# Five small loads moved from SyncE to ScalarE, and 26 filling products, at the start of an attention and routing kernel

## Chip, cores and metric

The kernel runs on one core of a Trainium2 chip. The time is that of the whole program on the device, in microseconds (us); lower is better. A time of a kernel is the median of several executions; one more execution was recorded by the profiler, and all rows of the trace come from that one.

## What is computed

Pooled attention is followed by a mixture of experts in which every token goes to one expert. Batch is 8, heads 8, sequence 576, head width 64; there are 8 experts, 4608 tokens of width 512, and 1024 hidden units per expert.

```python
k_p = k.reshape(B, H, Sp, 8, D).mean(axis=3)      # keys and values averaged over 8 rows
v_p = v.reshape(B, H, Sp, 8, D).mean(axis=3)
scores = scale * q @ k_p^T ; attn = softmax(scores) ; x = attn @ v_p
logits = x @ w_gate + modality_bias[modality_id]   # the five loads bring modality_id and modality_bias
e_idx = argmax(logits) ; gate_w = softmax(logits)[e_idx]
out[token] = gate_w * (relu(x @ w1[e_idx]) @ w2[e_idx])
```

## The kernel before

**Stages.** The attention takes the first 145 us or so. It runs in 20 steps, five for each pair of batches. A step takes one or two tiles of 128 queries: `q_pe` turns the queries (L679), `q_act` copies them out (L685), `s_pe` makes the scores (L704, L698), `s_dve` takes the maximum and subtracts it (L711, L714), `s_act` is the exponential (L726, L727), `t_pe` and `t_act` turn the weights (L733, L738), `a_pe` multiplies by the values (L768, L772), `x_dve` divides (L801). The rest of the span is the experts, on TensorE.

**Keys and values.** For each batch the 8 rows of a block are added up: by `fold` on GpSimd (POOL, L458 to L460) or by `reduce8` on VectorE (DVE, L463). `k_operand` then turns the pooled keys (L502, L507) and ScalarE copies them (L510, L511). `v_operand` lets ScalarE scale the pooled values (L542, L543), TensorE turn them (`pv`, L549: three transposes, u = 0, 1, 2) and ScalarE copy the result (L551). `gate_operand` (L444, L446) lays out the gate weights `wg` on GpSimd.

**Order.** Every engine runs its own instructions in the order in which the program lists them. SyncE (SP) issues all loads and stores: before the first step the loads of batches 0 and 1, the gate weights and one mixed tile of queries (L360 to L395, L439), then by `step_loads` what each step asks for. The five loads of `load_routing` stand in step 1, after the loads for q 2, k 3 and v 3 and before that for k 4. They bring the token's modality in two parts for each half of a batch pair (L583: 128 partitions by 4 pieces of 32 bytes; L585: 64 partitions by 4 pieces of 8 bytes) and the bias table for all partitions (L588: 128 pieces of 64 bytes). Their only reader is `modality_terms` on GpSimd in step 5 (L624 to L627).

**Turns.** The framework gives each load or store that SyncE or ScalarE issues one of eight completion semaphores, in turn over both engines in the order of its schedule, and a load first waits until the load that had its semaphore before it has landed.

**Filling.** `fill(n)` (L490) issues n products of 128 by 128 by 128 in bf16 on constants into a PSUM tile that nobody reads. The opening lines up to the step loop (L1070 to L1086) and two of its helpers have 58 of them (L494).

Of the kernel before, what the change touches and what calls it, by code (L numbers as in the profile page):

```python
# [9 lines left out]
F32 = mybir.dt.float32  # L10
# [12 lines left out]
P = 128  # L23
# [11 lines left out]
def kernel(  # L35
# [303 lines left out]
    with ExitStack() as actx:  # L339
# [150 lines left out]
        def fill(n):  # L490

            t = ps_av.tile([P, 2, 512], F32, tag="av", name="fill")
            for _ in range(n):
                nc.tensor.matmul(t[:, 0, 0:P], iota_b, iota_b, start=True, stop=True)  # L494

        def k_operand(b, i):
            kp, kp4 = kps[b]
            dst = kt[b % NB]
            pk = ps_tr.tile([64, 3 * P], F32, tag="tr", name=f"pk_{b}_{i}")
            cs = K_PART[i]  # L500
            for j, c in enumerate(cs):
                nc.tensor.transpose(pk[:, j * P:(j + 1) * P], kp[:, c, :], ident)  # L502
                if b == 0 and i == 0:
                    fill(5 if j else 20)
            n = len(cs) * P
            if i == 1:
                nc.tensor.transpose(pk[:, n:n + P], kp[:, NCH, :], ident)  # L507
                n += 64
            x = slice(cs[0] * P, cs[0] * P + n)
            nc.scalar.copy(dst[0:64, 0, x], pk[:, 0:n])  # L510
            nc.scalar.copy(dst[64:128, 1, x], pk[:, 0:n])  # L511
# [27 lines left out]
        def v_operand(b):  # L539
            vp, vp4 = vps[b]  # L540
            dw, d4 = vw[b % NB], v4[b % NB]
            nc.scalar.activation(dw[:, :, 0, 0:HD], vp[:, 0:NPAIR, :], AF.Copy, scale=m_a)  # L542
            nc.scalar.activation(dw[:, :, 1, 0:HD], vp[:, 0:NPAIR, :], AF.Copy, scale=m_b)  # L543
            (nc.gpsimd if b else nc.vector).tensor_tensor(d4[:, :, 0:HD], vp4.rearrange("p (o d) -> p o d", o=1).to_broadcast([P, NPAIR, HD]),
                                    m4b.to_broadcast([P, NPAIR, HD]), op=ALU.mult)

            pv = ps_tr.tile([P, 3, P], F32, tag="tr", name=f"pv_{b}")
            for u in range(3):
                nc.tensor.transpose(pv[:, u, :], vp[:, 2 * u:2 * u + 2, :], ident)  # L549
            vts[b] = ap.tile([P, 3, P], F32, tag="vt", bufs=1, name=f"vt_{b}")  # L550
            nc.scalar.copy(vts[b], pv)  # L551

# [21 lines left out]

        RC = {}

        def load_routing():

            mod = ap.tile([P, NT, 2], I32, name="mod")
            mv = modality.bitcast(I32).rearrange("(n w) -> n w", w=2)  # L580
            for z in range(2):
                mz = mv.rearrange("(i z s) w -> z i s w", z=2, s=S)[z]
                nc.sync.dma_start(mod.rearrange("p (i t) w -> p i (t w)", t=GT)[:, :, 10 * z:10 * z + 8],  # L583
                                  mz[:, 0:512, :].rearrange("i (p j) w -> p i (j w)", j=4))
                nc.sync.dma_start(mod.rearrange("p (i t) w -> p i t w", t=GT)[64 * z:64 * z + 64, :, 4, :],  # L585
                                  mz[:, 512:S, :].rearrange("i p w -> p i w"))
            mb = ap.tile([P, 2, E], F32, name="mb")
            nc.sync.dma_start(mb.rearrange("p m e -> p (m e)"),  # L588
                              modality_bias.rearrange("m e -> (m e)").rearrange("(o x) -> o x", o=1).to_broadcast([P, 2 * E]))
            RC.update(mod=mod, mb=mb)  # L590

        def routing_constants():
            ids = ap.tile([P, NT], I32, name="ids")
# [75 lines left out]
        def q_pe(n, w):  # L669
            b, jj, ts_ = steps[n]  # L670
            nq = 2 * len(ts_)
            qt = ap.tile([P, 4, P], F32, tag=f"qt{w}", bufs=1, name=f"qt_{n}_{w}")
            pq = ps_tr.tile([P, 4, P], F32, tag="tr", name=f"pq_{n}_{w}")
            for c in range(nq):
                if jj is None:
                    src = qmix[b // 2][:, 4 * w + 2 * c:4 * w + 2 * c + 2, :]
                else:
                    src = qpure[b][:, 4 * w + c, 2 * jj:2 * jj + 2, :]
                nc.tensor.transpose(pq[:, c, :], src, ident)  # L679
            qts[n, w] = qt  # L680
            pqs[n, w] = pq[:, 0:nq, :]

        def q_act(n, w):
            pq = pqs.pop((n, w))
            nc.scalar.copy(qts[n, w][:, 0:2 * len(steps[n][2]), :], pq)  # L685
# [62 lines left out]
        def t4_act(n):  # L748

            dst = pt4s[n]  # L750
            for z in range(len(steps[n][2])):
                nc.scalar.copy(pt4z[z][64 * z:64 * z + 64], dst[64 * z:64 * z + 64])  # L752
# [298 lines left out]

        step_loads = {}
        for n, fn, b in ((0, load_k, 2), (0, load_k4, 2), (0, load_v, 2), (0, load_v4, 2), (1, load_q, 2), (1, load_k, 3),
                         (1, load_v, 3), (1, load_k4, 3), (1, load_routing, None), (1, load_k, 4), (2, load_qmix, 1),
                         (2, load_v4, 3), (2, load_v, 4), (3, load_k4, 4), (4, load_q, 3), (4, load_k, 5), (4, load_v4, 4),
                         (4, load_v, 5), (5, load_k4, 5), (5, load_k, 6), (6, load_q, 4), (6, load_v4, 5), (6, load_v, 6),
                         (7, load_qmix, 2), (7, load_k4, 6), (7, load_k, 7), (9, load_q, 5), (9, load_v4, 6), (9, load_v, 7),
                         (10, load_k4, 7), (11, load_q, 6), (11, load_v4, 7), (12, load_qmix, 3), (14, load_q, 7)):
            step_loads.setdefault(n, []).append((fn, b))
# [11 lines left out]
        k_operand(0, 0)  # L1071
        q_pe(0, 0)
        q_act(0, 0)
        fill(6)
        s_pe(0, 0)
        fill(14)
# [1 line left out]
        s_dve(0, 0)  # L1078
        token_ids()
        k_operand(0, 1)  # L1080
        q_pe(0, 1)
        q_act(0, 1)
        pool_v(0)
        gate_operand()
        fill(8)
        s_act(0, 0)  # L1086

        def run(hook, n):
            for fn in hook.get(n, ()):
# [7 lines left out]
        for n in range(N + 1):  # L1097
            has, nxt, nxt2 = n < N, n + 1 < N, n + 2 < N
            old = steps[n - 1][2] if n else ()
            two = len(old) > 1  # L1100
            ahead = two and has and steps[n][1] is None
            loads(n)
            run(hook_0, n)
            if old:
                t_pe(old[0])
                t_act(old[0])
                if has:
                    s_act(n, 0)
            if has:
                s_pe(n, 1)  # L1110
            if due:
                release()
            if old:
                t4_pe(n - 1)
                t4_act(n - 1)
            if n == N:
                run(hook_3, N - 1)
            if ahead:
                t_pe(old[1])
                t_act(old[1])  # L1120
            if n == 2:
                a_pe(old[0])
            run(hook_1, n)
            if old and n != 2:
                a_pe(old[0])
            if has:
                s_dve(n, 1)
            finish()
            if n == 0:
                q_pe(1, 0)  # L1130
                q_act(1, 0)
                v_operand(0)
            if two and not ahead:
                t_pe(old[1])
                t_act(old[1])
            if n == 1 or n == 2:
                q_pe(n + 1, 0)
                q_act(n + 1, 0)
            if nxt:
                q_pe(n + 1, 1)  # L1140
            run(hook_q, n)
            if old:
                x_dve(old[0])
            if n == N - 2:
                finish()
            gap(2)
            if nxt and n:
                q_act(n + 1, 1)
            if has:
                s_act(n, 1)  # L1150
            if n == 0:
                q_act(n + 1, 1)
            if n == 1:
                pool_k_rest(1)
                pool_v_rest(1, 2)
                a_pe(old[1])
                x_dve(old[1])
            if n == 2:
                pool_k_rest(2, 2)
            if nxt:  # L1160
                s_pe(n + 1, 0)
            if nxt2 and n > 1:
                q_pe(n + 2, 0)
                q_act(n + 2, 0)
            if nxt:
                s_dve(n + 1, 0)
            if n == 2:
                pool_k_rest(2)
            if n == 0:
                v_gate(0)  # L1170
                pool_k(1)
            run(hook_2, n)
            finish()
            due = bool(drip) and drip[0] in held
            if two and n != 1:
                a_pe(old[1])
                x_dve(old[1])
            gap(2)
            if n != N - 1:
                run(hook_3, n)  # L1180
            finish()
# [557 lines left out]
```

## Time and profile before

| | us |
|---|---|
| median of three executions | 581.89 |
| lowest and highest of the three | 579.84, 583.59 |
| the profiled execution, its own time | 581.18 |
| its span in the trace, first to last instruction | 579.5 |
| TensorE busy in it | 562.1 (97%) |
| mean granted TensorE clock | 0.996 |

The profiled execution lies 0.7 us under the median, and 1.7 us of its time lie outside the span. Times in the trace count from the start of the span. PE is TensorE, PEld its weight loads, DVE VectorE, ACT ScalarE, POOL GpSimd, SP SyncE; SPq is an instruction of SyncE's own queue, here the issue of a load. A tile's name stands without its number: `qt` is any of the query tiles. The granted clock is a share of 2.4 GHz, so 0.50 is 1.2 GHz.

### The profile page before, as it was taken

The page shows a single profiled execution, that of the slowest core. Times are in us where ns is not written, and L with a number is a line of the kernel's source. Part 1 is how long each engine was busy: PE and PEld are TensorE (multiplying, and loading weights), DVE is VectorE, ACT ScalarE, POOL GpSimd, SP SyncE. Part 2 cuts the span into 40 slices and gives each one's busy share as a digit, 9 for nine tenths or more (in the row PEclk, how much of TensorE's full clock was granted, in tenths as well). Part 3 has the DMA queues.
Part 4 walks back from the last instruction along what each step waited for, and adds up shares of the span by engine and source line. Part 5 has one row for each costly group of instructions (what it writes and reads, how often), then busy time and mean ns, then how long its engine had stood idle before and what let it go on. Part 6 is the DMA issues. An engine that isn't in the chain of part 4 may idle for free.

```text
span 579.5 us, 12256 instructions
## 1 busy us (share of the span) xinstructions
PE 562.1 (97%) x3487; PEld 494.5 (85%) x3487; DVE 372.7 (64%) x947; ACT 270.7 (47%) x656; POOL 183.6 (32%) x292
## 2 busy tenths in 40 slices
PE   4999999999999999999999999999999999999996
PEld 4889889899898888888888888888888888888894
DVE  5887888778878786567455446855455588455311
ACT  2667667789752443334333336533333474334210
POOL 6679987854201302202202102022112113212102
PEclk9899999999999999999999999999999999999999
DMA  8998999994431533232232277233234853242001
GB/s 249 279 332 251 358 334 281 338 274 164 166 94 43 153 101 111 79 105 94 92 110 95 89 236 244 93 114 94 87 114 129 241 205 108 91 133 74 26 21 56
DMA packets 80940, 90.69 MB, mean 157 GB/s; under 512 B 17935, under 2 KB 56335, under 8 KB 80848
## 3 DMA queue, kind: packets, MB, share of 16 engines
q1 hardware_dynamic: 74928, 70.14, 39.3%
q0 software_dynamic: 5920, 19.44, 10.3%
q8 instruction: 43, 0.70, 0.5%
q14 instruction: 49, 0.40, 0.3%
HBM read 115.72 MB, written 28.62 MB: 249 GB/s over the span
## 4 chain that ended last, share of the span: by engine, by line
PE 90%; DVE 3%; DMA 2%; ACT 2%; issue 1%; SPq 1%; POOLq 0%; ACTq 0%; DVEq 0%
PE op L1436 34%; PE hp L236 20%; PE hp L240 10%; PE av L768 6%; PE sc L704 4%; PE av L772 3%; PE hp L193 3%; PE pq L679 3%; PE pp L733 2%; PE ph L193 2%; DMA q<-in_q_dram 2%; DMA out_dram<-obw,slw 1%; PE sc L698 1%; PE pk L502 1%; PE sc L561 1%
## 5 line engine op out<-in xcount | busy, mean ns | idle before, releaser
L236 PE MATMUL hp<-xhl,hl 128*128 128x512 f32 (+1 forms) x512 | 146.5, 388 | 0.1
L1412 POOL DMA_INDIRECT out_dram<-ob,sidx x34 | 35.4, 1041 | 275.6 <-DVE ob L1406 204.7
L257 DVE TENSOR_TENSOR ht<-ht,hp 128x256 f32<-128x256 f32 x128 | 52.9, 419 | 99.7 <-ACT ht L256 88.0
L256 ACT COPY ht<-hp 128x256 f32<-128x256 f32 x128 | 47.1, 372 | 129.8 <-PE hp L236 124.4
L1436 PE MATMUL op<-hl,hx 128*128 128x512 f32 x429 | 103.5, 389 | 0.0
L236 PEld LDWEIGHTS hp<-xhl,hl 128*128 128x128 f32 x512 | 87.0, 188 | 10.3 <-issue 0.5
L1436 PEld LDWEIGHTS op<-hl,hx 128*128 128x128 f32 x429 | 80.4, 188 | 16.3
L240 PEld LDWEIGHTS hp<-xhl,hl 128*128 128x128 f32 x512 | 78.1, 189 | 9.9
L240 PE MATMUL hp<-xhl,hl 128*128 128x256 f32 (+1 forms) x512 | 80.7, 280 | 0.0
L1436 PE MATMUL op<-hl,hh 128*128 128x512 f32 x256 | 78.8, 389 | 0.0
L1436 PEld LDWEIGHTS op<-hl,hh 128*128 128x128 f32 x256 | 48.0, 188 | 9.8
L1436 PE MATMUL op<-hl,hlo 128*128 128x512 f32 x128 | 49.8, 389 | 0.0
L768 PE MATMUL av<-vw,pt 128*128 128x146 f32 (+1 forms) x320 | 48.9, 292 | 0.7 <-DVE xb L801 0.6
L151 POOL DMA_INDIRECT xg<-xs,gidx x36 | 38.0, 1054 | 17.3 <-issue 10.1
L768 PEld LDWEIGHTS av<-vw,pt 128*128 128x128 f32 (+1 forms) x320 | 39.6, 180 | 2.5 <-ACT pt L752 0.8
L704 PE MATMUL sc<-kt,qt 128*128 128x144 f32 x256 | 37.9, 292 | 0.4 <-ACT qt L685 0.4
L262 DVE SCALAR_TENSOR_TENSOR hx<-ht,hx 128x256 fp32r<-128x256 f32 x64 | 27.1, 425 | 16.1 <-DVEq L1441 14.3
L262 DVE SCALAR_TENSOR_TENSOR hlo<-ht,hh 128x256 fp32r<-128x256 f32 x64 | 27.0, 424 | 16.1 <-DVEq L1441 13.7
L704 PEld LDWEIGHTS sc<-kt,qt 128*128 128x128 f32 x256 | 34.1, 195 | 0.8 <-issue 0.6
L711 DVE TENSOR_REDUCE mx<-sc 128x8 f32<-128x576 f32 (+1 forms) x40 | 27.6, 691 | 6.8 <-PE sc L704 6.3
L260 ACT ACTIVATE hx<-ht 128x256 fp32r<-128x256 f32 x64 | 26.5, 420 | 10.1 <-DVE ht L257 10.0
L772 PE MATMUL av<-vw,pt 128*128 128x146 f32 (+1 forms) x160 | 30.3, 291 | 0.2
(281 smaller groups left out, 899.5 us busy)
## 6 DMA issues: line engine op xcount, KB each, us to landing
raw<-in_moe_w_dram SPq DMA_DIRECT2D x256, 256.0 KB
scr<-xg SPq DMA_DIRECT2D x35, 256.0 KB
xs<-xb SPq DMA_DIRECT2D x16, 528.0 KB
k<-in_k_dram SPq DMA_DIRECT2D x7, 1024.0 KB
v<-in_v_dram SPq DMA_DIRECT2D x7, 1024.0 KB
q<-in_q_dram SPq DMA_DIRECT2D x7, 1024.0 KB
y<-scr SPq DMA_DIRECT2D x108, 64.0 KB
v<-in_v_dram SPq DMA_DIRECT2D x16, 128.0 KB
```

Source lines behind the costliest of these rows:

```text
L151: nc.gpsimd.indirect_dma_start(out=x, out_offset=None, in_=xs[0:rows, :], in_offset=IndirectOffsetOnAxis(idx[:, col:col + 1].bitcast(U32), 0),
L193: nc.tensor.matmul(ph[:, 0:width], hl[f][:, w, d * P:(d + 1) * P], ab[:, 1 - x, d, 0:width], start=(n == 0 and d == 0), stop=(n == 2 and d ...
L236: nc.tensor.matmul(ph[:, :, 0:n], hl[g][:, 0, d * P:(d + 1) * P], ab[:, :, d, 0:n], start=(d == 0), stop=(d == ND - 1))
L240: nc.tensor.matmul(ph[:, 1, 0:n], hl[g][:, 1, d * P:(d + 1) * P], ab[:, 1, d, 0:n], start=False, stop=False)
L256: nc.scalar.copy(hts[g % 2], hp[g % 2][:, 0:SLOT])
L257: nc.vector.tensor_add(hts[g % 2], hts[g % 2], hp[g % 2][:, SLOT:2 * SLOT])
L262: nc.vector.scalar_tensor_tensor(hlo, hts[g % 2], 0.0, hh.bitcast(F32), op0=ALU.max, op1=ALU.subtract)
L704: nc.tensor.matmul(dst, qt[:, i, :], kt[b % NB][:, :, h * SPL:(h + 1) * SPL], start=True, stop=True)
L768: nc.tensor.matmul(av[hs, u, 2 * VC * gg:2 * VC * (gg + 1)], pt[:, c, hs], vw[y][:, c].rearrange("p a x -> p (a x)"), start=(gg == 0), sto ...
L772: nc.tensor.matmul(dst4[hs], pt4[:, hs], v4[y][:, 2 * u:2 * u + 2, :], start=False, stop=True)
L1412: nc.gpsimd.indirect_dma_start(out=out[:, :], out_offset=IndirectOffsetOnAxis(idx.bitcast(U32), 0), in_=ob, in_offset=None, bounds_check=N ...
L1436: nc.tensor.matmul(ot, l[:, ts_], hl[f][:, w, D:2 * D], start=(f == 0 and n == 0), stop=(f == NF - 1 and n == 2))
```

## The change

`load_routing` is taken out of step 1 of SyncE's list and cut into three functions whose loads ScalarE issues. After the first `q_act` ScalarE issues the first half's large part, the bias and the first half's small part; after the first `s_act` the second half's large part; in step 1, behind `t4_act`, the second half's small part. Sizes and targets of the loads stay as they are. Sixteen filling products are added behind `k_operand(0, 1)` and ten in `v_operand(0)`, behind its first transpose.

```diff
             for u in range(3):
                 nc.tensor.transpose(pv[:, u, :], vp[:, 2 * u:2 * u + 2, :], ident)
+                if b == 0 and u == 0:
+                    fill(10)
...
-        def load_routing():
...
-                nc.sync.dma_start(mod.rearrange("p (i t) w -> p i (t w)", t=GT)[:, :, 10 * z:10 * z + 8],
-                                  mz[:, 0:512, :].rearrange("i (p j) w -> p i (j w)", j=4))
...
+        def load_mod(z):
...
+            nc.scalar.dma_start(RC["mod"].rearrange("p (i t) w -> p i (t w)", t=GT)[:, :, 10 * z:10 * z + 8],
+                                mz[:, 0:512, :].rearrange("i (p j) w -> p i (j w)", j=4))
+
+        def load_mod4(z):
...
+            nc.scalar.dma_start(RC["mod"].rearrange("p (i t) w -> p i t w", t=GT)[64 * z:64 * z + 64, :, 4, :],
+                                mz[:, 512:S, :].rearrange("i p w -> p i w"))
+
+        def load_bias():
...
-                         (1, load_v, 3), (1, load_k4, 3), (1, load_routing, None), (1, load_k, 4), (2, load_qmix, 1),
+                         (1, load_v, 3), (1, load_k4, 3), (1, load_k, 4), (2, load_qmix, 1),
...
         q_act(0, 0)
+        load_mod(0)
+        load_bias()
+        load_mod4(0)
         fill(6)
         s_pe(0, 0)
...
         k_operand(0, 1)
+        fill(16)
         q_pe(0, 1)
         q_act(0, 1)
         pool_v(0)
         gate_operand()
         fill(8)
         s_act(0, 0)
+        load_mod(1)
...
                 t4_act(n - 1)
+            if n == 1:
+                load_mod4(1)
```

## Rows read from the trace of the kernel before

**Rows 1.** Chain that ended last, 13 to 24 us (start, length, what).
```profile
5.75 8.84 DMA q<-in_q_dram
```

**Rows 2.** Waits of PE, 28 us to the end (total, times, longest).
```profile
PE ph L193 <- ACT pt L738: 0.7, 1, 0.7
PE av L768 <- DVE xb L801: 0.6, 1, 0.6
PE pq L679 <- ACT qt L685: 0.4, 1, 0.4
PE pv L549 <- DVE vp L463: 0.3, 1, 0.3
```

**Rows 3.** Windows: stretch, length, busy PE PEld DVE ACT POOL, PEclk, DMA, GB/s.
```profile
12.60:14.60 2.00, 0.00 (x0) 0.00 (x0) 1.97 (x3) 0.62 (x2) 1.92 (x3) 1.00 1.11 271
14.85:18.20 3.35, 3.35 (x20) 3.20 (x19) 2.22 (x5) 1.32 (x3) 2.44 (x5) 0.50 1.11 298
```

**Rows 4.** Timeline of PE: start, length, what, count [idle before, releaser].
```profile
10.34 1.22 PE L704 MATMUL sc<-kt,qt 128*128 128x144 f32 x8 [0.43 <-ACT qt L685]
11.40 0.94 PE L494 MATMUL fill<-iota_b 128*128 128x128 bf16 x14
...
14.63 0.96 PE L679 MATMUL pq<-ident,q 128*128 128x128 f32 x4 [2.07 <-DMA q<-in_q_dram]
...
16.27 2.20 PE L704 MATMUL sc<-kt,qt 128*128 128x144 f32 x8
...
46.91 0.41 PE L549 MATMUL pv<-ident,vp 128*128 128x128 f32 x2 [0.26 <-DVE vp L463]
```

**Rows 5.** Timeline of ACT.
```profile
12.60 0.31 ACT L510 COPY kt<-pk 64x192 f32<-64x192 f32 x1 [2.40 <-PE pk L507]
...
19.01 0.58 ACT L685 COPY qt<-pq 128x512 f32<-128x512 f32 x1 [2.05 <-PE pq L679]
19.49 0.51 ACT L542 ACTIVATE vw<-vp,m_a 128x256 f32<-128x256 f32 x1
...
25.89 0.58 ACT L738 COPY pt<-pp 128x512 f32<-128x512 f32 x1 [1.50 <-PE pp L733]
```

**Rows 6.** Timeline of SP: issues of loads and how long each took.
```profile
21.05 2.05 SPq L357 DMA_DIRECT2D k<-in_k_dram  x1
...
39.80 0.58 SPq L583 DMA_DIRECT2D mod<-in_moe_modality_id_dram  x1
...
42.36 2.86 SPq L585 DMA_DIRECT2D mod<-in_moe_modality_id_dram  x1
...
47.10 0.56 SPq L357 DMA_DIRECT2D k<-in_k_dram  x1
```

**Rows 7.** Timeline of POOL.
```profile
11.77 0.73 POOL L458 TENSOR_TENSOR v<-v 128x256 f32<-128x256 f32 x1 [2.95 <-DMA v<-in_v_dram]
...
16.73 0.73 POOL L458 TENSOR_TENSOR v<-v 128x256 f32<-128x256 f32 x1 [0.67 <-DMA v<-in_v_dram]
...
18.07 0.32 POOL L460 TENSOR_TENSOR vp<-v 128x64 f32<-128x64 f32 x1
...
18.58 0.47 POOL L444 COPY wgb<-wg 64x32 f32<-64x32 f32 x2
...
21.17 1.26 POOL L458 TENSOR_TENSOR k<-k 128x512 f32<-128x512 f32 x1 [1.86 <-DMA k<-in_k_dram]
...
34.88 1.28 POOL L458 TENSOR_TENSOR k<-k 128x512 f32<-128x512 f32 x1 [3.13 <-DMA k<-in_k_dram]
...
45.36 0.32 POOL L460 TENSOR_TENSOR vp<-v 128x64 f32<-128x64 f32 x1
```

**Rows 8.** Windows as in Rows 3, for the DMA share and rate at the end.
```profile
16.00:17.50 1.50, 1.50 (x10) 1.41 (x8) 0.90 (x2) 0.95 (x3) 0.79 (x2) 0.50 1.04 364
17.50:22.50 5.00, 4.48 (x35) 4.14 (x34) 3.15 (x6) 3.37 (x9) 2.77 (x7) 0.92 1.19 180
...
44.50:48.50 4.00, 3.65 (x28) 3.20 (x28) 3.57 (x5) 3.92 (x11) 3.69 (x7) 1.00 0.59 97
```

More of the change, by code (lines that the diff above doesn't have):

```diff
@@ L575 @@
         RC = {}
-        def load_routing():
-            mod = ap.tile([P, NT, 2], I32, name="mod")
+        RC.update(mod=ap.tile([P, NT, 2], I32, name="mod"), mb=ap.tile([P, 2, E], F32, name="mb"))
+        def load_mod(z):
             mv = modality.bitcast(I32).rearrange("(n w) -> n w", w=2)
-            for z in range(2):
-                mz = mv.rearrange("(i z s) w -> z i s w", z=2, s=S)[z]
-                nc.sync.dma_start(mod.rearrange("p (i t) w -> p i (t w)", t=GT)[:, :, 10 * z:10 * z + 8],
-                                  mz[:, 0:512, :].rearrange("i (p j) w -> p i (j w)", j=4))
[L585 to L590, printed above, removed]
+            mz = mv.rearrange("(i z s) w -> z i s w", z=2, s=S)[z]
+            nc.scalar.dma_start(RC["mod"].rearrange("p (i t) w -> p i (t w)", t=GT)[:, :, 10 * z:10 * z + 8],
+                                mz[:, 0:512, :].rearrange("i (p j) w -> p i (j w)", j=4))
+        def load_mod4(z):
+            mv = modality.bitcast(I32).rearrange("(n w) -> n w", w=2)
+            mz = mv.rearrange("(i z s) w -> z i s w", z=2, s=S)[z]
+            nc.scalar.dma_start(RC["mod"].rearrange("p (i t) w -> p i t w", t=GT)[64 * z:64 * z + 64, :, 4, :],
+                                mz[:, 512:S, :].rearrange("i p w -> p i w"))
+        def load_bias():
+            nc.scalar.dma_start(RC["mb"].rearrange("p m e -> p (m e)"),
+                                modality_bias.rearrange("m e -> (m e)").rearrange("(o x) -> o x", o=1).to_broadcast([P, 2 * E]))
         def routing_constants():
```

## The prediction

> **What bounds the kernel now.** I read the chain of work that ended last first. It begins with a transfer, the second half of batch 0's queries, 8.84 us from its issue to the transposes at 14.63 us that it releases [rows 1], and from there runs almost wholly over TensorE. The waits of TensorE from 28 us to the end come to 2.0 us in four entries, and none of the four is for a transfer [rows 2]. So a microsecond can be won or lost for the whole kernel only where TensorE still waits, in the first 25 us, or where something new makes it wait.
>
> Then I looked at the stretch around 14.63 us. From 12.60 to 14.60 TensorE does nothing, and from 14.85 to 18.20 its clock is granted at 0.50, the lower of its two levels, 1.2 GHz [rows 3]. Eight score products that take 1.22 us at 10.34, behind an idle time of 0.43 us, take 2.20 us at 16.27, after the idle time of 2.07 us [rows 4]. That is what the filling products can repair.
>
> Third, the transfers. The DMA share is over 1 in every window read up to 22.5 us [rows 3, 8], and GpSimd waits for transfers until batch 2's keys start it at 34.88 us [rows 7]. So early on a byte or a piece that is put ahead of others delays them. By then batch 2's keys set GpSimd, and GpSimd's pooled values of batch 2, which end at 45.36 + 0.32 = 45.68 us [rows 7], are read by the last of three transposes; the last two of them start at 46.91 us [rows 4]. The cushion there is 46.91 - 45.68 = 1.2 us.
>
> **The change part by part.** *SyncE loses five issues.* They hold its queue from 39.80 until the next load is issued at 47.10, 7.3 us [rows 6]. Behind them stand the load of batch 4's keys and all later loads and stores. But TensorE has no wait for a transfer after 28 us [rows 2], so nothing that ends late depends on these being early: 0, and no loss either, since only waiting time of SyncE goes. The reader of the five loads runs after 47 us in any case.
>
> *ScalarE gains five issues.* An issue took SyncE 0.58 to 2.86 us [rows 6]; the long ones came with a crowded queue, so I take 0.6. Three stand in a gap of 2.40 us that ends at 12.60 [rows 5], 1.8 us of issue. With semaphores in turn, I expect them to wait for the short values of batch 0, which landed by 11.77 [rows 7]; then they end at 11.8 + 1.8 = 13.6, and the key copies due at 12.60 are 1.0 us late. What needs those next is the score products at 16.27 [rows 4], so it costs nothing; at 2.86 us each (11.8 + 8.6 = 20.4 us) it would cost 20.4 + 0.6 - 16.3 = 4.7 us, an end that I think far off. The fifth falls into a gap of 1.50 us before 25.89 [rows 5]: 0 at 0.6, up to 1.4 at 2.86.
>
> The fourth is the delicate one. It stands in the gap of 2.05 us before the query copy at 19.01, from where ScalarE works without a pause and TensorE waits for it. By count it is the 21st issue and waits for the 13th, the gate weights' second half. These have landed when GpSimd copies them without a wait at 18.58 [rows 7]; I estimate 18.2. ScalarE is held until then, and 0.6 more.
>
> *The pieces in the queues.* The loads are 1664 pieces of at most 64 bytes. The rate falls from 364 GB/s to 180 for the 5 us from 17.5 [rows 8], when the gate weights (1024 pieces of 32 bytes) and the mixed queries (1024 of 256 bytes) pass: 5 x (1 - 180/364) = 2.5 us lost. Shared over all 2048 that is 1.2 ns a piece, put on the gate weights alone 2.5 ns; so 1664 pieces cost 2.1 to 4.1 us of all queues. From the other side, where the five loads pass now, 44.5 to 48.5 us, the share is 0.59, 2.4 us of queue time, of which 97 GB/s x 4 us at 364 GB/s is 1.1 us: 1.3 us for the pieces [rows 8]. No row shows two hardware queues at once, so pieces from the second could also slip between the others for 0. I take 1.5 us for all five, nearest to the row of these very loads, and about half of it, 0.8, for the first three (896 pieces). Today that time falls into the hole at 44.5 us, in the future into the full queues before 34.88 us. Of 1.5 us the cushion of 1.2 hides all but **0.3 us** (0 if the pieces are free, 2.9 at 4.1 us).
>
> The Trainium skill, in "DMA: Bandwidth & Descriptors" under "Queues, rings and completion order", says that each DMA engine serves the queues that have work in turn, a packet at a time; under "Issuing engines are not separate DMA queues" it adds that issuing from several engines saves only issue time. By that rule the new loads don't stand behind SyncE's backlog but cut into it, and the critical query half would land some 0.5 us later; if they queued behind, it would land as now. The rule speaks against this change, and no run here shows which holds.
>
> *Twenty-six filling products.* At 0.94 us for 14 [rows 4] they cost 0.067 us each. Sixteen take 1.07 us of the idle 2.07 us before 14.63, off the path, and leave 1.0 us idle, or 1.5 if the queries are 0.5 us later. The clock held after 0.43 us idle and fell after 2.07; I take it to hold. Then the transposes and the score products lose their doubled time (2.20 - 1.22 = 1.0 us, and 0.3 to 0.4 for the transposes). But batch 0's pooled values come from GpSimd at 18.07 + 0.32 = 18.39 after a transfer at 16.73 [rows 7], and ScalarE's scaling of them, now at 19.49 [rows 5], can't start before 18.45: of 1.4 us 1.04 are left. Ten products stand between the first and the second transpose of these same values, 0.67 us on the path. So the filling wins 1.04 - 0.67 = **0.4 us**, no more.
>
> *The sum at 19 us.* Best: -0.4. Against it the fourth load: gate weights 18.2, + 0.6 for the pieces ahead of them, + 0.6 of issue = 19.4 for a copy due at 19.01, +0.4; with a late landing (18.8 + 1.1 + 0.6 = 20.5) +1.5. The held copy also takes away the -0.4, for everything on ScalarE follows it. I take **+0.4**. The 0.3 at 46 us is not added: TensorE that is late by 0.4 arrives later there too, and only the larger of the two counts. 581.18 + 0.4 = 581.6 for an execution like the profiled one; the median of the three lay 0.7 us higher, and I forecast half-way, **582.0 us**.
>
> **The rivals**, in the same frame. *The loads ride free and the clock holds.* The gate weights land early in the gap, or the turn falls on an earlier semaphore, and the pieces slip between. For it: ScalarE's three gaps (2.40, 2.05, 1.50 us) are each longer than their issues at 0.6 us. Against it: the full queues. Then -0.4: 581.2.
>
> *The clock falls all the same.* The query half comes late enough that the idle time is again near 2 us, or 1.0 us is enough. Then nothing is won at 16 us, while the ten products and the held copy stay: 0.4 + 0.8 = +1.2, 582.8.
>
> *ScalarE is held by a large load.* This is the slower side. A load waits for the one that had its semaphore; if one of the first three gets its turn behind batch 1's keys, which land only at 21.17 us (SyncE's next user of that turn was let go at 21.05) [rows 6, 7], ScalarE stands from 12.60 - 2.40 = 10.2 to 21.2, the key copies (0.6 us) end behind a last issue at 21.2 + 0.6 + 0.6 = 22.4, and the score products due at 16.27 come 6.1 us late: 588.1. It decides from the point where a load's turn comes eight or more issues behind batch 1's keys. For it: SyncE's own queue shows such waits. Against it: batch 1's keys are the 14th load on SyncE's list, so the three should come right behind them and wait for the 7th to the 9th.
>
> **How the numbers follow.** Forecast 0.45, loads free 0.35, clock falls 0.10, ScalarE held 0.08, a gain of over 1% from something that I don't see 0.02. The range takes in the free case with the best end of the sum and some 1 us for the scatter of a median whose three runs span 3.7 us, 581.2 - 1.4 = 579.8; above, 581.6 + 2.9 for the dear pieces with 0.7 for the median, 585.2. It leaves out the held case. A measurement of this kernel can tell a change from none at about 1%, 5.8 us: only the held case and the unseen gain go beyond it, and part of the first two's tails: faster 0.02, same 0.90, slower 0.08.
>
> **What would show it.** In the profile after: five issues on ScalarE's queue, at about 0.6 us each, the fourth ending near 19.4; the granted clock at 1.00 from 14.85 to 18.20, and eight score products near 1.2 us there; the query half landing at about 15.1; GpSimd's start on batch 2's keys at 36.4 instead of 34.88; SyncE's load of batch 4's keys some 7 us earlier with nobody the better for it; and a wait of TensorE or VectorE for the pooled values near 47 us. The forecast is wrong if the start on batch 2's keys does not move (the pieces are free), if the clock still falls, or if ScalarE stands at an issue for more than 2 us. It is also wrong if TensorE's waits after 28 us shrink below the 2.0 us, for I give the freed SyncE nothing.

## The result and the profile after

The changed kernel takes 587.13 us in the median of seven runs (584.62 to 589.30); the kernel before took 581.89 us beside it (579.51 to 583.59). That is 5.2 us slower between the medians, and outside the range of the prediction. The ratio of the two kernels is 1.0104, with a 95% interval of [1.0081, 1.0127] (intervals stand in this form below), which is 4.7 to 7.4 us. The profiled execution took 589.30 us, the longest of the seven, with a span of 587.5 us.

I looked first at the timeline of ScalarE in the profile of the changed kernel, because the prediction named it as the engine to watch (start, length, what, count, idle time before and what ended it).

```profile
11.55 0.45 ACTq L585 DMA_DIRECT2D mod<-in_moe_modality_id_dram  x1
12.05 0.51 ACTq L597 DMA_DIRECT2D mb<-n_moe_modality_bias_dram  x1
13.02 0.69 ACTq L592 DMA_DIRECT2D mod<-in_moe_modality_id_dram  x1
13.75 0.31 ACT L510 COPY kt<-pk 64x192 f32<-64x192 f32 x1 [3.03 <-PE pk L507]
...
16.31 0.31 ACT L735 ACTIVATE pe<-sb 128x64 f32<-128x64 f32 x1
21.19 0.39 ACTq L585 DMA_DIRECT2D mod<-in_moe_modality_id_dram  x1
21.68 0.58 ACT L693 COPY qt<-pq 128x512 f32<-128x512 f32 x1 [5.06 <-DMA k<-in_k_dram]
...
27.49 0.60 ACTq L592 DMA_DIRECT2D mod<-in_moe_modality_id_dram  x1
```

The first three loads behave as forecast. At the fourth ScalarE stands from 16.62 to 21.19 us, and what lets it go is a load of keys. The query copy that stood at 19.01 before [rows 5] comes at 21.68. GpSimd names the keys: it starts adding up batch 1's keys at 21.31, at the same moment.

```profile
21.31 1.26 POOL L458 TENSOR_TENSOR k<-k 128x512 f32<-128x512 f32 x1 [1.68 <-DMA k<-in_k_dram]
...
33.47 1.27 POOL L458 TENSOR_TENSOR k<-k 128x512 f32<-128x512 f32 x1 [2.97 <-DMA k<-in_k_dram]
```

On TensorE, as in [rows 4]:

```profile
12.92 1.05 PE L494 MATMUL fill<-iota_b 128*128 128x128 bf16 x16
14.60 0.66 PE L687 MATMUL pq<-ident,q 128*128 128x128 f32 x4 [0.63 <-DMA q<-in_q_dram]
...
15.93 1.25 PE L712 MATMUL sc<-kt,qt 128*128 128x144 f32 x8 [0.23 <-ACT qt L693]
...
18.48 0.44 PE L549 MATMUL pv<-ident,vp 128*128 128x128 f32 x2 [0.20 <-POOL vp L460]
22.32 1.12 PE L687 MATMUL pq<-ident,q 128*128 128x128 f32 x4 [3.40 <-ACT qt L693]
23.23 2.06 PE L712 MATMUL sc<-kt,qt 128*128 128x144 f32 x8
...
25.72 0.63 PE L741 MATMUL pp<-ident,pe 128*128 128x128 f32 x4
```

The same stretch in windows (columns as in [rows 3]):

```profile
14.85:18.20 3.35, 3.12 (x35) 2.83 (x33) 2.74 (x6) 1.32 (x3) 2.50 (x5) 1.00 1.04 301
18.20:21.60 3.40, 0.52 (x4) 0.20 (x2) 1.32 (x3) 0.00 (x0) 1.54 (x6) 1.00 1.09 172
21.60:22.20 0.60, 0.00 (x0) 0.00 (x0) 0.00 (x0) 0.52 (x2) 0.60 (x1) 0.57 1.05 321
22.20:25.10 2.90, 2.78 (x12) 2.78 (x13) 0.00 (x0) 2.40 (x7) 2.67 (x5) 0.50 1.05 346
25.10:28.00 2.90, 2.86 (x26) 2.64 (x24) 2.56 (x5) 2.04 (x7) 1.97 (x4) 1.00 1.14 313
```

The filling does its work: the clock is at 1.00 from 14.85 to 18.20, where it was 0.50 [rows 3], and the eight score products take 1.25 us for 2.20. Then TensorE stands for 3.40 us behind ScalarE, and at the end of that wait the clock falls. So the low clock is back, at 0.50 from 22.20 to 25.10. The first transposes of the attention weights start at 25.72; before they started at 21.98, so 3.7 us are lost by there. The transposes at 46.91 [rows 4] are now at 50.74, 3.8 us later, the first product of the experts (`ph`) is at 160.40 for 155.86, 4.5 us later, and a scatter of GpSimd at 463.31 for 458.77, still 4.5. So most of the loss arises between 16.6 and 25.7 us. Of the waits of TensorE from 28 us to the end, these are new against [rows 2]:

```profile
PE hp L236 <- DVE ht L257: 2.0, 1, 2.0
...
PE sc L753 <- DVE sb L722: 0.5, 1, 0.5
...
PE sc L706 <- ACT vg L570: 0.4, 1, 0.4
```

The two small ones stand at 73 and 74 us, where the loss grows from 3.8 to 4.7. They do not belong to the hold alone: both also stand, at 0.5 us each, in the profiles with the products alone and with fifteen products and not the ten (below), where ScalarE is not held. The first is a stop at 479 us, for which see the last section.

**The turn.** The prediction counted the fourth load as the 21st issue of SyncE and ScalarE together. Counted in the order of the changed program's schedule it is the 22nd (in brackets the issue whose landing it waits for):

```
turn       both: 13th  SyncE, gate weights, second half
                 14th  SyncE, batch 1's keys
           15th to 17th  ScalarE, its first three loads
           18th to 20th  SyncE, batch 1's last key rows, mixed queries (two)
with sixteen products                       with fifteen products
21st  SyncE, batch 1's values (for 13th)    ScalarE, fourth load (for 13th)
22nd  ScalarE, fourth load (for 14th)       SyncE, batch 1's values (for 14th)
```

The trace bears the table out, because its records name the semaphore of every issue: eight of them, numbered 100 to 107. In the change the fourth load has 105. Batch 1's keys had 105 before it; the last of them landed at 21.17 us, and ScalarE's issue follows 0.02 us later. With fifteen products (below) the fourth load has 104, which the second half of the gate weights had before it. I take it that the sixteen products make TensorE, and through it the exponential ahead of the fourth load, later in the schedule, so that the load of batch 1's values slips ahead; the runs show the order, not how the schedule comes to it.

My theory: the loss is this standing of ScalarE before the fourth load (the hold), by one turn. The rivals: the loads on ScalarE cost by themselves (pieces, issue time), or the added products do.

### The profile page after: what moved, and what is told of

It is laid out like the page before. It is cut to its first block, busy times and chain, and to the rows that moved or that the text cites. A ratio compares the mean times of both kernels' runs of the same rounds, so it can differ in the third digit from the quotient of the medians.

```text
span 587.5 us, 12306 instructions
## 1 busy us (share of the span) xinstructions
PE 565.2 (96%) x3513; PEld 496.9 (85%) x3513; DVE 372.4 (63%) x947; ACT 270.9 (46%) x656; POOL 184.3 (31%) x292
## 4 chain that ended last, share of the span: by engine, by line
issue 25%; PE 16%; DMA 11%; POOL 1%; DVE 1%; POOLq 0%; DVEq 0%
DMA out_dram<-ob,sidx 9%; PE op L1451 8%; PE hp L236 4%; PE hp L193 3%; PE hp L240 2%; DMA xg<-xs,gidx 1%; DMA out_dram<-obw,slw 1%; POOL xg L151 1%; POOL out_dram L1427 0%; DVE xg L304 0%; POOLq L1749 0%; DVE obw L1647 0%; DVE ob L1421 0%; POOLq L1427 0%; POOLq L151 0%
## 5 line engine op out<-in xcount | busy, mean ns | idle before, releaser
L719 DVE TENSOR_REDUCE mx<-sc 128x8 f32<-128x576 f32 (+1 forms) x40 | 27.6, 691 | 11.1 <-PE sc L712 10.4
```

The source lines that it names most:

```text
L719: nc.vector.reduce_max(mx, scv, axis=AX.X)
```

## The experiments

Each group of runs had the kernel before on the same chip; its medians were 581.28, 580.91 and 580.48 us in the three groups, in the order below (four kernels, four, three).

**One product less.**

```diff
-        fill(16)
+        fill(15)
```

> The changed kernel with fifteen filling products behind k_operand(0, 1) in place of sixteen; all else is as in the change, and the load order is such that the fourth load of ScalarE takes its turn ahead of the load of batch 1's values, so that it is the 21st issue and waits for the 13th, the second half of the gate weights, in place of the 14th, batch 1's keys. Turn theory (ScalarE stands at the fourth load until batch 1's keys have landed, and TensorE's clock falls while it waits): the copy that came at 21.68 us comes near 19, the score products behind it run at the full clock, and the time falls by 2.7 + 1.4 = 4.1 us from 587.1 to about 583. Traffic theory (the 1664 small pieces among the early transfers cost the time): stays at 587 within 0.5. Filling theory (the products between the transposes and the clock cost it): 587 less 0.07 us.

Measured: 580.47 us, ratio 0.9979 [0.9959, 0.9999]. ScalarE issues the fourth load at 16.29, 0.5 us behind the end of the exponential; the gate weights' second half, for which it now waits, landed at 16.27. The query copy is not late by that, it follows TensorE's transposes:

```profile
16.29 0.40 ACTq L585 DMA_DIRECT2D mod<-in_moe_modality_id_dram  x1
16.88 0.58 ACT L693 COPY qt<-pq 128x512 f32<-128x512 f32 x1 [1.09 <-PE pq L687]
```

SyncE's load of batch 1's values, which is now the 22nd, is issued at 19.80 and waits for the keys in ScalarE's place (waits of SyncE's queue: total, times, longest):

```profile
SPq L372 <- DMA k<-in_k_dram: 2.9, 1, 2.9
```

There it costs nothing. One filling product is worth 5.2 + 0.8 = 6.0 us, each against the kernel before on its own chip. All five loads and 25 of 26 products stay, so neither rival holds the loss. It came out better than expected, see below.

**The products alone**: all 26, and the five loads left on SyncE in step 1.

> The kernel before with the 26 filling products and nothing else; SyncE issues the five loads in step 1 as before. Turn theory: no hold, the clock stays up from 14.85 to 18.20 us, so 581.9 less 0.4, between 580.9 and 582. Traffic theory: the same, about 581.5. Filling theory: 586 to 587, the whole loss.

Measured: 580.64 us, 0.9996 [0.9976, 1.0015]. The granted clock from 14.60 to 18.50 is 1.00. So the products show no loss by themselves.

**The fourth load later**: it moves from behind the first `s_act` to step 1, ahead of the fifth.

```diff
         s_act(0, 0)
-        load_mod(1)
...
             if n == 1:
+                load_mod(1)
                 load_mod4(1)
```

> The changed kernel with the fourth load moved from behind the first s_act to step 1, just ahead of the fifth, where its turn is behind loads that have long landed. Turn theory: no hold at 16.6 us, the gain of the filling stays, 581 to 582. Traffic theory: the pieces still run among the early transfers, only 512 of them some 7 us later, so 586 to 587. Filling theory: 586 to 587.

Measured: 581.79 us, 1.0002 [0.9983, 1.0021]. The load is issued at 22.90, and no query copy of ScalarE waits for a transfer.

**The hold alone.** The loads stay on SyncE; behind the first `s_act` ScalarE copies one value of batch 1's keys, so that it must wait for them.

```diff
         s_act(0, 0)
+        hk = ap.tile([1, 1], F32, name="hk")
+        nc.scalar.copy(hk, kraw[1][0:1, 0, 0:1])
```

> The kernel before with the 26 filling products, the five loads on SyncE in step 1 as before, and one more instruction on ScalarE behind the first s_act: a copy of one value of batch 1's keys into a tile that nobody reads, so ScalarE stands there until those keys have landed. Nothing else is moved. Turn theory: about 587, the loss of the change with none of its loads. Traffic theory: as with the filling alone, about 581.5. Filling theory: 586 to 587 as with the filling alone.

Measured: 584.57 us, 1.0059 [1.0034, 1.0083]: a loss of 3.3 us with no load moved, but short of the 587 that I expected. ScalarE, and below it TensorE:

```profile
19.51 0.19 ACT L1091 COPY hk<-k 1x1 f32<-1x1 f32 x1 [3.55 <-DMA k<-in_k_dram]
...
20.23 0.66 PE L681 MATMUL pq<-ident,q 128*128 128x128 f32 x4 [1.99 <-ACT qt L687]
20.72 1.15 PE L706 MATMUL sc<-kt,qt 128*128 128x144 f32 x8
...
22.56 0.66 PE L735 MATMUL pp<-ident,pe 128*128 128x128 f32 x4
```

This hold is shorter than the change's (3.55 for 5.06 us), TensorE stands 1.99 for 3.40 us, and here the clock does not fall. That fits with its giving only part of the 5.2 us; the next section divides the rest.

**The change again**, on the chip of the next three.

> The change as it is, beside the three kernels that follow. If the place of its loss is the hold of ScalarE at its fourth load, this profile shows it again: a wait of 4 to 5.5 us on ScalarE that ends with batch 1's keys, an idle time of TensorE of 2 to 3.5 us before the transposes of batch 0's third query tile, and 586 to 588 us. The late stop of 2 us at 479 us that the first profile of the change showed has nothing to do with it by this theory and should not come again; then the span is some 584 us. If the late stop belongs to the change, it stands here again near 479 us and the span is near 587.5 us.

Measured: 585.82 us, 1.0096 [1.0062, 1.0130]; span 583.3 us. The hold and the low clock are there once more, the stop at 479 us is not:

```profile
20.79 0.58 ACT L693 COPY qt<-pq 128x512 f32<-128x512 f32 x1 [5.25 <-DMA k<-in_k_dram]
...
21.43 1.12 PE L687 MATMUL pq<-ident,q 128*128 128x128 f32 x4 [3.31 <-ACT qt L693]
22.34 2.13 PE L712 MATMUL sc<-kt,qt 128*128 128x144 f32 x8
```

**Forty products into the hold.**

```diff
                 v_operand(0)
+                fill(40)
```

> The change with forty filling products more, behind the transposes of batch 0's values, where TensorE stood idle for 3.40 us while ScalarE was held. At 0.067 us each they fill 2.7 us of it. The hold stays. Theory: the price of the hold is the wait itself and, behind it, the lower clock, which made the four transposes take 1.12 in place of 0.66 us and the eight score products 2.06 in place of 1.15 us, 1.37 us in all; with the idle time filled the clock stays at 1.00 and the kernel takes 1.4 us less than the change on the same chip, about 585.7. Rival: the clock's part is hidden behind ScalarE, which is busy from the end of the hold to the first transposes of the weights; then the time is that of the change, within 0.5 us.

Measured: 587.31 us, 1.0090 [1.0058, 1.0122]. The expected 1.4 us did not show. In the profiled execution the keys came late, and TensorE stood for 3.06 us all the same, behind the products:

```profile
18.28 2.40 PE L494 MATMUL fill<-iota_b 128*128 128x128 bf16 x40
23.73 0.66 PE L687 MATMUL pq<-ident,q 128*128 128x128 f32 x4 [3.06 <-ACT qt L693]
24.23 1.35 PE L712 MATMUL sc<-kt,qt 128*128 128x144 f32 x8
25.38 1.33 PE L563 MATMUL pg<-wgb,vt 128*128 128x32 f32 x6
```

The clock falls later, in the products behind the scores (granted 0.50 from 25.40 to 27.40). Forty were too few, and the run decides nothing on the clock's share.

**The loads alone**: the change without `fill(16)` and `fill(10)`.

> The change without any of its 26 filling products. Without the sixteen the fourth load gets its turn one place earlier, behind the second half of the gate weights and not behind batch 1's keys. Theory of the turn: no hold on ScalarE, although all five loads stand where the change puts them; the clock falls at 14.6 us as in the kernel before, and the time is that of before, 0.5 us less to 0.5 us more. Rival, that loads on ScalarE's queue cost by themselves, by pieces that cut into the big transfers or by the hold at whatever load comes before them: 584 us or more, with ScalarE standing for 2 us or more at the fourth load.

Measured: 581.08 us, 1.0003 [0.9983, 1.0023]. ScalarE issues the fourth load at 17.74, 0.12 us behind the end of the exponential (the gate weights' second half landed at 17.72); no hold to speak of. That refutes the rival of the loads. One part of the expectation missed: in the profiled execution the clock had fallen earlier (eight score products at 11.74 took 2.26 us) and was up again by 16.92.

**Fifteen products and not the ten.**

> The change with fifteen in place of sixteen products and without the ten. No hold, as with fifteen and ten (580.47 us). The ten stand on TensorE's path at 17 us and cost 0.7 us there; if nothing behind them gives the time back, this kernel takes 0.3 to 0.7 us less than that one, 579.8 to 580.2. If the ten keep the clock up in the wait for the pooled values, or if what is won before 20 us is given back by 155 us anyhow, it takes the same or up to 0.5 us more.

Measured: 580.79 us, 0.9990 [0.9974, 1.0007]: the same as with the ten. Without them TensorE waits at the same place, for GpSimd's pooled values, which end at 17.27 + 0.32 = 17.59 us (GpSimd, then TensorE):

```profile
17.27 0.32 POOL L460 TENSOR_TENSOR vp<-v 128x64 f32<-128x64 f32 x1
...
17.64 0.44 PE L549 MATMUL pv<-ident,vp 128*128 128x128 f32 x2 [0.79 <-DVE mx L717]
```

The row names VectorE, whose maximum (`mx`) ends at 17.61, in the same moment. The transposes do not read that maximum; they read the pooled values, of which GpSimd's are the last. Either way TensorE would have waited there, so the ten stand in a wait of 0.79 us and cost nothing.

**Fifteen products, and the turn shifted back.** SyncE's load of batch 1's last key rows is made as two loads, of 32 rows each.

```diff
-            nc.sync.dma_start(k4raw[b], rows_of(k, b)[NCH * P:, :])
+            for r in (range(0, 64, 32) if b == 1 else (0,)):
+                m = 32 if b == 1 else 64
+                nc.sync.dma_start(k4raw[b][r:r + m], rows_of(k, b)[NCH * P + r:NCH * P + r + m, :])
```

> The version with fifteen products, which took 580.47 us and showed no hold, with one thing more: the load of batch 1's last 64 key rows, which SyncE issues right behind batch 1's keys, is made as two loads of 32 rows each. Same bytes, same products; one issue more ahead of ScalarE's fourth load, which becomes the 22nd again and gets its turn behind batch 1's keys. Theory of the turn: the hold is back, ScalarE stands 4 us or more before the fourth load and is let go by batch 1's keys, first transposes of the weights at 24.5 to 26.5 us, 585 to 587 us. Rival, that the sixteenth product itself or the work of TensorE makes the loss: no hold and 580 to 581.5 us.

Measured: 585.50 us, 1.0086 [1.0067, 1.0105]. The hold is back with the products that had none:

```profile
19.66 0.39 ACTq L587 DMA_DIRECT2D mod<-in_moe_modality_id_dram  x1
20.15 0.59 ACT L695 COPY qt<-pq 128x512 f32<-128x512 f32 x1 [4.77 <-DMA k<-in_k_dram]
...
20.79 0.66 PE L689 MATMUL pq<-ident,q 128*128 128x128 f32 x4 [3.24 <-ACT qt L695]
```

The first transposes of the weights start at 23.58, 0.9 us earlier than expected. The sum of bytes and of products is that of the 580.47 us version; only the number of issues differs.

**Sixteen products, and a small load in the 14th place.**

```diff
-        load_k(1)
         load_k4(1)
+        load_k(1)
```

> The change with all its products, and SyncE issues the load of batch 1's last key rows ahead of batch 1's keys and not behind them. The fourth load stays the 22nd and waits for the 14th, but the 14th is now the small one of the two, 256 KB for 1024. Theory of the turn: no wait for batch 1's keys; ScalarE issues the fourth load between 16 and 18.5 us, TensorE has no idle time over 1.5 us there, and the time is 580.5 to 582.5 us, near that of before. Its first three loads move one turn as well, and the third of them then waits for the second half of batch 0's queries, so the key copies may come 1 to 2 us later and cost up to 1 us. Rival, that sixteen products on this path bring the loss whatever the fourth load waits for: 585 us or more.

Measured: 581.73 us, 1.0019 [1.0000, 1.0038]. The fourth load still has semaphore 105 and waits for the 14th issue, but that one, now the small load, lands at 17.66, and the clock stays up:

```profile
17.68 0.41 ACTq L585 DMA_DIRECT2D mod<-in_moe_modality_id_dram  x1
18.19 0.59 ACT L693 COPY qt<-pq 128x512 f32<-128x512 f32 x1 [1.54 <-DMA k<-in_k_dram]
...
18.83 0.66 PE L687 MATMUL pq<-ident,q 128*128 128x128 f32 x4 [0.29 <-ACT qt L693]
```

Batch 1's own keys land later here (GpSimd starts on them at 21.82), so this wait for `k` is for the small load. The third load waits for the query half as expected and ends at 13.93 + 0.68 = 14.61; the key copies are late by it, and TensorE waits 0.90 us ahead of the scores at 15.95. This and the run before settle the theory from both sides: the hold comes and goes with what stands in the 14th place, with fifteen products and with sixteen.

**Eighty products into the hold.**

> The change with eighty products where forty stood in the run before, 4.8 us at 0.060 us each, so that TensorE is busy until 22.5 to 23 us, past the end of the hold in two of the three profiles so far. Theory: the clock stays at 1.00 behind the hold, so from the held transposes to the first transposes of the weights it takes 2.2 to 2.3 us as without a hold, where the change took 3.40 and 3.60; the products themselves can run up to 1.5 us past the end of the hold and eat that gain, so the whole is 584.5 to 586. Rival, that the clock falls behind a hold in any case: 3.4 us or more between those two, and 586.5 to 588.

Measured: 586.80 us, 1.0101 [1.0073, 1.0129]. The time lies 0.8 us over the upper end of the first expectation and inside the rival's 586.5 to 588; the rows speak against the rival on the interval that it named, and the window below them gives the clock (columns as in [rows 3]):

```profile
17.64 4.63 PE L494 MATMUL fill<-iota_b 128*128 128x128 bf16 x80
22.11 0.61 PE L687 MATMUL pq<-ident,q 128*128 128x128 f32 x4
22.55 1.15 PE L712 MATMUL sc<-kt,qt 128*128 128x144 f32 x8
...
24.12 0.63 PE L741 MATMUL pp<-ident,pe 128*128 128x128 f32 x4
```

```profile
22.00:23.70 1.70, 1.70 (x20) 1.70 (x17) 0.00 (x0) 1.18 (x3) 1.54 (x4) 1.00 1.06 358
```

From the held transposes to the first transposes of the weights it takes 24.12 - 22.11 = 2.0 us at a clock of 1.00, for 25.72 - 22.32 = 3.40 and 3.60 us in the two profiles of the change. So the hold and the low clock are two costs in this stage, and the second can be kept away; that the whole kernel gains by it no run shows. Part of the difference comes from ScalarE, which was let go at 19.61 and so was well ahead of the transposes; with the hold alone, at the same clock, it takes 2.33 us. The transposes could have started 1.1 us behind 19.61, at 20.7 (as in the change, 21.19 to 22.32); the products end over an us later and eat the gain. Behind the first transposes of the weights this execution loses a further 1.6 us against the change until `ph` (160.46 - 24.12 = 136.3 us for 134.7), and why was not settled.

## Why the prediction was wrong

**The step that failed** is "By count it is the 21st issue and waits for the 13th, the gate weights' second half". The count took the kernel's order without what the sixteen products do to the schedule: with them the load of batch 1's values stands ahead, and the fourth load becomes the 22nd and waits for the 14th, batch 1's keys. ScalarE stood for 4.6 us (16.62 to 21.19), and the forecast +0.4 for the query copy (19.4 for 19.01) became +2.7 (21.68).

**The mechanism was among the rivals**, at another load. I priced "ScalarE is held by a large load" for "one of the first three" and gave it 0.08. Its condition, "a load's turn comes eight or more issues behind batch 1's keys", is met by the fourth to the issue: 22 - 14 = 8. Its argument against, that the three come right behind the keys, was right for the three and was not asked of the fourth. For a load whose turn is one away from a large one that case needed far more than 0.08. That its 588.1 lies near the measured 587.13 is luck: it was worked out for the first three loads and for score products 6.1 us late.

**The price of the hold.** From the query half's transposes to the first transposes of the weights it takes 25.72 - 14.60 = 11.1 us in the change and 19.86 - 13.77 = 6.1 us with fifteen products: 5.0 us. The parts, taken against the run with the hold alone (22.56 - 13.95 = 8.6 us): its wait for the keys costs 2.5; in the change the keys land 1.0 us later behind the queries (21.19 - 14.60 = 6.6 for 19.51 - 13.95 = 5.6); issue and restart of TensorE take 0.4 more (22.32 - 21.19 = 1.13 for 20.23 - 19.51 = 0.72); and the lower clock takes 3.40 - 2.33 = 1.1. That sums to 5.0. Each is from one execution, and landings differ by an us between executions, so the first two parts are rough. The medians give 6.0 for the change (5.2 and 0.8 won) and 5.8 for the split loads (5.0 and 0.8); the part beyond 5 us is not placed. The two small waits at 73 us may take some of it; they stand in all six profiles with a hold, but also in two of the six of my kernels without one.

**The fourth load without the hold.** As the 21st issue it does wait for the gate weights' second half, as I had said, but these land earlier than my 18.2: at 16.27 with fifteen products, at 16.33 without the ten, at 17.72 with the loads alone, and at 17.02 in the kernel before. Each time the issue follows 0.02 us later, so ScalarE stands for 0.5, 0.6 and 0.1 us, and the query copy, which waits for TensorE's transposes, is not late by it. My 18.2 came from GpSimd's copy at 18.58 [rows 7], which is an upper bound only: GpSimd was at work on the values until then. With 0 in place of +0.4 the likeliest case was that of the free loads, 581.2, which 580.47 and 580.79 bear out.

**The filling.** I took the clock to hold and gave -0.4 us. It held. In the stage it wins more: 6.1 us for 7.35 before (21.98 - 14.63), 1.3 us, because the 0.67 us of the ten products lie in a wait and not on the path. Of this 0.8 us are left in the medians with fifteen products (the interval of the ratio gives 0.1 to 2.4), and with the products alone it is nothing that can be told from zero (0.9996 [0.9976, 1.0015]). Where the rest goes back I did not settle; in the run with fifteen TensorE's waits after 28 us come to 3.0 us in five entries instead of 2.0 [rows 2].

**The first three loads** went as forecast: wait until 11.55, last issue ended at 13.71 for 13.6, key copies 1.15 us late for 1.0, at no cost to the scores (15.93 for 16.27 before). **Issues** took 0.39 to 0.69 us; I took 0.6. **The fifth** cost nothing. **SyncE** issued the load of batch 4's keys at 38.10 for 47.10 [rows 6], 9 us earlier, and nothing is better for it: the loads alone give 1.0003.

**The pieces** were to make GpSimd start on batch 2's keys at 36.4. It started at 33.47, earlier than before [rows 7]. In the other kernels with the five loads on ScalarE it started at 32.23 to 34.31, but for the forty products into the hold (35.60, where batch 1's keys landed 1.4 us later than in the change); in the two of my kernels with the loads on SyncE it started at 33.41 and 33.59. None reached 36.4, and in this scatter no price of the pieces can be seen: the case near the lower end of my bounds was the right one. The packets of ScalarE's queue took 1.2 us of all 16 engines in the change, near the 1.5 that I took. One reading behind it was wrong: the slow 5 us from 17.5 are not the gate weights', whose pieces passed from 13.17 to 16.00 in the kernel before; so the 2.1 to 4.1 us, which count them in, had no ground.

**The query half.** Its transposes started at 14.60 for 14.63, not at 15.1. This single pair says little: over the runs they started at 13.36 to 15.59 with the loads on ScalarE, and at 13.95 to 15.53 with them on SyncE. The pieces did not stand behind SyncE's backlog: ScalarE's first load, issued at 11.55, landed at 17.53, ahead of batch 1's keys, which SyncE had issued at 11.09 and which landed at 21.17. That agrees with the rule of the Trainium skill ("DMA: Bandwidth & Descriptors", "Queues, rings and completion order") that the engines serve the queues in turn. The 0.5 us by which I made the query half later with it, a figure for which the prediction shows no working, can be neither seen nor excluded in that scatter. Under "Issuing engines are not separate DMA queues" the same page of the Trainium skill says that another issuing engine saves issue time only, and the 0 for SyncE agrees with that. In this kernel the new issuer also takes over the wait for a turn: 4.6 us on ScalarE.

**Best version.** Fifteen products with all else of the change, 0.9979 [0.9959, 0.9999], is the fastest of those run, and by less than a measurement of this kernel can tell well.

## What to carry to other kernels

In this framework a load moved to a computing engine brings its wait for a completion semaphore with it, and what it waits for is set by its place in the count of all issues, not by its size. Count the turns in the order that the changed program really has, with all its edits in it: here one product of 0.067 us, or one load made as two, put a 1 MB load into the wait and cost 5 to 6 us. Where a large load stands next to the one counted, treat both as open, or move the small load to a place where its engine can stand (step 1: 1.0002).

## What was not expected of the hardware

In four profiles the hold left TensorE idle for 3.06 to 3.40 us, and each time its clock fell to 0.50, the level of 1.2 GHz: in the change between 21.60 and 22.20 us, while it was still idle, in the split version only at about 22.3, when it had been at work again for 1.5 us (granted 1.00 from 21.40 to 22.00, 0.55 from 22.00 to 22.60). After 1.99 us (the hold alone) and 0.63 us (the query half in the change) it did not fall. In the kernel before it fell behind 2.07 us [rows 3, 4], and with the loads alone behind 1.79 us (ahead of the transposes at 10.32; granted 0.50 from 11.00 to 14.00); so an idle time near 2 us is seen with both outcomes.

The first profile of the change also shows a stop that is not the hold's. At 476.49 VectorE starts 2.54 us late on gathered rows, and TensorE behind it:

```profile
476.49 0.76 DVE L304 TENSOR_TENSOR xg<-xg 128x256 f32<-128x256 f32 x2 [2.54 <-DMA xg<-xs,gidx]
...
479.11 0.76 PE L236 MATMUL hp<-xhl,hl 128*128 128x512 f32 x1 [2.01 <-DVE ht L257]
...
480.00:482.00 2.00, 2.00 (x8) 1.71 (x8) 2.00 (x4) 1.75 (x2) 0.00 (x0) 0.50 0.11 35
```

The clock is at 0.50 from 480 to 482 us. TensorE's longest wait for this tile was 0.3 to 1.3 us in nine of the eleven profiles of the experiments, with the hold and without it; none stands in those of before, of the hold alone and of the change again. So it is taken as this execution's own; it was not tested.
